# Layer one of two MLP layers: f tiles of two blocks in another order, and three more pairs of them by seven products

## The chip, the cores and the metric

One of the cores of a Trainium2 chip runs the whole program. A core has engines that each work through their own list of instructions in order: TensorE (PE in the profile; PEld is its weight load), VectorE (DVE), ScalarE (ACT), GpSimd (POOL) and SyncE (SP, which here issues DMAs). They wait for each other by semaphores. The metric is the device time of one execution in microseconds, less is better.

## The reference, cut to what matters

Three stages follow each other, in float32:

```
x = attention(q, k, v, lam)                # 2 batches x 768 tokens x 512
u = x + real(fft(fft(x, axis=tokens), axis=features))
un = layernorm(u)
u = u + relu(un @ w1) @ w2                 # layer one, w1 512x2048, w2 2048x512
xn = layernorm(u) * g
out = u + relu(xn @ w1b) @ w2b             # layer two, same sizes
```

The attention is a retention with a decaying state over 12 chunks of 64 tokens (the kernel goes by chunks of 128). The change touches layer one alone.

## The kernel before, in words

Numbers are kept as pairs of float16 (a high part and the rest), so a product of two matrices is three passes of matmuls. The tokens are cut in four blocks of 384: block 0 and 1 are batch 0, block 2 and 3 batch 1 (the two halves of a batch come out of one transform by symmetry). The Fourier step is done by matmuls with tables: for batch 1, `ps_pq1_0` to `ps_pq1_2` hold its results for the token tiles 0 to 2; L594 and L596 are its last matmuls for a tile, L631 adds them to `u`.

A layer goes over its blocks in turn, and in a block over 16 f tiles of 128 hidden features. One unit of the program is one f tile of one block: the up-projection of tile f (`w1`), the relu, and the down-projection (`w2`) of the tile that was begun LAG = 3 units earlier, which adds to three accumulators `ps_y` of 128x512 in PSUM for the whole block. The last tile of a block closes the accumulators (`stop`, in `down_mm`) and adds them to `u` (`drain`, L1021).

The up-projection has two forms:

- The slow form, `mlp_up` (L745 to L756): 12 matmuls of 384 columns for one f tile (L755), so 24 for two tiles. Then ACT takes the relu to float16 (L769) and DVE the rest (L770), once for each tile.
- Seven products, `mlp_up_fast` and `pair_prod` (L842 to L909, all matmuls on L864): two f tiles are taken together as a 2x2 block product, 7 products of 6 matmuls of 192 columns. It needs sums of weights (`sw`, `w1_sums`, L788 to L800) and of the block's input (`th`, `un_sums`, L806 to L839: two `tr` by L811, four DVE operations on `ts`, the casts L828 on ACT and the rests L829 on POOL, all of it twice, for kk = 0 and 1). It also needs work between the products, in PSUM: ACT copies the first product (L880), DVE forms `u2` (L881) and `u3` (L888) and adds (L889, L894, L895); then two relu on ACT (L900) and two rests on DVE (L901). Two of these bind the order. After `u3` has been read out of the left bank's second half (L888), that half is overwritten by the next product:

```
prod(left[:, HB:TB], 3, 3)
prod(left[:, :HB], "12", "21")
dve.tensor_tensor(u3, left[:, HB:TB], m1, op=ALU.add)                  # L888
dve.tensor_tensor(right[:, HB:TB], right[:, :HB], u3, op=ALU.add)      # L889
def rest():                                                            # after the unit's down-projection
    prod(left[:, HB:TB], "22", 4)
```

In layer one, `fast_from` says from which f tile on a block goes by seven products: none of blocks 0 and 1, block 2 from f = 4 (F02), block 3 from 0. All of layer two goes by them.

The input of a block comes from the layer norm: DVE takes statistics (L689, L692, L695), POOL a power (L697), DVE the shift (L708), ACT normalises (L709) and casts (L717), POOL forms the rest (L718), and SP issues the DMA transposes of both parts into `unT` (L720).

`put(n, task)` places such side work at unit n of the program. What each engine does in which order is settled when the program is built: the tile framework's timeline scheduler goes by the order in which the code was written as priority and by its own estimate of durations. At run time each engine keeps that order.

Of the kernel before, what the change touches and what calls it, by code (L numbers as in the profile page):

```python
# [19 lines left out]
P = 128  # L20
# [4 lines left out]
NF = DF // P  # L25
# [23 lines left out]
e0 M12 N12 M20 M21 N20 r0 e1 e0 f0 M22 N21 r1 f0 N22 r2  # L49
"""  # L50
ONPOOL = "Y2"
EARLY0, GATEN, B1, SPC, DS, DC, DFO, DD, D1S, D2S, AO, YA, NR, NE, LN1, L1, L2, F01, F02, TL, R1, R2, SE, PR1, LAG, UB, FB, NW, MQ, SPL = 11, 8, 6, 2.0, 2.0, 5, 1.0, 0.5, 0.5, 1.0, "aba", "aa", 2, 0, 3, 2.5, 2.5, 16, 4, 3, 1.5, 2, "dddd_dppp", 0, 3, 3, 13, 11, 1, 3

SUMS = {(1, 0): 16, (1, 1): 18, (2, 0): 20, (2, 1): 25, (3, 0): 35, (3, 1): 38, (0, 0): 41, (0, 1): 43}

# [71 lines left out]
def tile_retention_fourier_mlp(ctx: ExitStack, tc: tile.TileContext, a: dict, out: bass.AP):  # L127
    nc = tc.nc
    pe, act, dve, pool, sp = nc.tensor, nc.scalar, nc.vector, nc.gpsimd, nc.sync
# [673 lines left out]
    def un_sums(m, blk, kk):  # L803
        run(un_sum_steps(m, blk, kk))

    def un_sum_steps(m, blk, kk):  # L806
        x = unT[m, blk]
        r = []
        for k in (kk, kk + 2):
            t = f32t(f"tr{m}_{blk}_{k}")[:, :TB]  # L810
            dve.tensor_tensor(t, x[:, 0, k], x[:, 1, k], op=ALU.add)  # L811
            yield t
            r += [t[:, :HB], t[:, HB:]]
        b11, b12, b21, b22 = r
        both = [f32t(f"ts{y}_{m}_{blk}_{kk}")[:, :TB] for y in (12, 34)]
        (t1, t2), (t3, t4) = ((z[:, :HB], z[:, HB:]) for z in both)
        tw[m, blk, kk] = []

        def pair(y):
            z = both[y]  # L820
            if (m, blk) == (1, 0):
                t = csp.tile([P, 2, NS], F16, tag=f"cs{2 * kk + y}", name=f"th{y}_{m}_{blk}_{kk}")[:, :, :TB]
            elif (m, blk) == (1, 2):
                t = tops[1 + y].rearrange("p n two -> p (n two)") if kk else wtp.tile([P, 512], F32, tag="wt", name=f"th{y}_{m}_{blk}_{kk}").bitcast(F16)
                t = t.rearrange("p (y n) -> p y n", y=2)[:, :, :TB]
            else:
                t = hl(f"th{y}_{m}_{blk}_{kk}")[:, :, :TB]
            act.copy(t[:, 0], z)  # L828
            pool.tensor_tensor(t[:, 1], z, t[:, 0], op=ALU.subtract)  # L829
            tw[m, blk, kk].append(t)  # L830

        dve.tensor_tensor(t1, b12, b11, op=ALU.subtract)
        yield t1
        dve.tensor_tensor(t2, b22, t1, op=ALU.subtract)
        pair(0)
        yield t2
        dve.tensor_tensor(t3, b22, b12, op=ALU.subtract)
        yield t3
# [72 lines left out]
    def down_mm(m, blk, f, part, first=0):  # L911
        j, c, ps = part
        h, w = hts[m, blk, f], w2t[m, f]
        for n, (x, y) in enumerate(PASS):
            pe.matmul(ps, h[:, x, j * P:(j + 1) * P], w[:, y, c], start=f == first and n == 0, stop=f == NF - 1 and n == 2,  # L915
                      skip_group_check=True)

    vsum, hsum, acc = {}, {}, {}
# [28 lines left out]
    def seven_mm(m, blk, f):  # L947
        p = f // 2
        h, w = [hts[m, blk, 2 * p + i] for i in range(2)], [w2t[m, 2 * p + i] for i in range(2)]
        one, two = slice(0, P), slice(TB - P, TB)  # L950
        (t1, t2), (t3, t4) = ([z[:, :, c] for c in (LEFT, RIGHT)] for z in vsum[p])
        (_, _, c1), (_, _, c2) = dn[blk][:2]
        ca, cb = acc["a"], acc["b"]
        if f % 2 == 0:
            todo = [(ca, LEFT, h[0][:, :, one], w[0][:, :, LEFT], 1), (c1, LEFT, h[1][:, :, one], w[1][:, :, LEFT], 1),
                    (c2, LEFT, h[1][:, :, two], t4, 1)]
        else:
            (s1, s2), (s3, s4) = ([z[:, :, x * P:x * P + P] for x in range(2)] for z in hsum.pop((blk, p)))
            todo = [(ca, RIGHT, s1, t1, 0), (cb, LEFT, s2, t2, 1), (cb, RIGHT, s3, t3, 0), (c1, RIGHT, s4, w[1][:, :, RIGHT], 0)]
        for ps, c, lhs, rhs, start in todo:  # L960
            for n, (x, y) in enumerate(PASS):
                pe.matmul(ps[:, c], lhs[:, x], rhs[:, y], start=start == 1 and n == 0 and p == 0, stop=n == 2,  # L962
                          skip_group_check=True)
        down_mm(m, blk, f, dn[blk][2])
# [42 lines left out]
    def mlp_down(m, blk, f):  # L1007
        if f == 0:
            dn[blk] = [(j, WHOLE, bank("dn", f"ps_y{m}_{blk}_{j}")) for j in range(3)]
        for part in dn[blk]:  # L1010
            down_mm(m, blk, f, part)
        if f == NF - 1:
            for i in range(3):
                drain(m, blk, i)

    def drain(m, blk, i):
        b, mir = divmod(blk, 2)
        j, _, ps = dn[blk][i]
        u = U[b][mir * 3 + j]
        if m == 0:  # L1020
            dve.scalar_tensor_tensor(u, ps, YS, u, op0=ALU.mult, op1=ALU.add)  # L1021
            return
        o = f32t(f"o{blk}_{j}")
        dve.scalar_tensor_tensor(o, ps, YS, u, op0=ALU.mult, op1=ALU.add)
        if not mir:
            sp.dma_start(out[b, j * P:(j + 1) * P, :], o)
            return
        od = dram.tile([P, DM], F32, name=f"od{blk}_{j}")
        sp.dma_start(od, o)
        n0 = 1 if j == 0 else 0  # L1030
# [292 lines left out]
    with tc.manual_schedule(engines={mybir.EngineType.PE, mybir.EngineType.DVE, mybir.EngineType.Pool, mybir.EngineType.Activation}):  # L1323
        for z in ORDER.split():
# [3 lines left out]
            if z[0] == "W":  # L1328
                ps = bank("up", f"warm{len(warm)}")
# [18 lines left out]
    def put(n, task):  # L1348
        bg.setdefault(max(int(n), 0), []).append((n, len(bg), task))
# [27 lines left out]
    n = t + DC + DFO  # L1377
# [11 lines left out]
    order = [[0, 1, 2, 3], [0, 1, 3, 2]]  # L1389
# [14 lines left out]
    first = {}  # L1404
# [18 lines left out]

    def step(n):
        m = n // (NB * NF)
        return m, order[m][n // NF % NB], n % NF

    fast_from = {(0, 2): F02, (0, 3): 0}
    fast_from.update({(1, blk): 0 for blk in range(NB)})
    for (m, blk), f in fast_from.items():  # L1430
        if (m, blk) in ((1, 3), (1, 2)):
            continue
        for kk in range(2):
            if m == 0 and blk < 3:
                put(16 * blk + f / 2 + kk - 3, lambda blk=blk, kk=kk: un_sums(0, blk, kk))
            else:
                at = m * NB * NF + order[m].index(blk) * NF
                put(at - TL + 2 * kk if (m, blk) != (1, 0) else at - 7 + 2 * kk, lambda m=m, blk=blk, kk=kk: un_sums(m, blk, kk))
# [3 lines left out]
    def unit(n):  # L1442
        rest = None
        if n < total:
            m, blk, f = step(n)
            if n >= SPL:
                rest = (mlp_up if f < fast_from.get((m, blk), NF) else mlp_up_fast)(m, blk, f)
        for _, _, task in sorted(bg.pop(n, ()), key=lambda z: z[0]):
            after("dve", lambda: after("act", task)) if n < GATEN else task()
        if n >= LAG:  # L1450
            mlp_down(*step(n - LAG))
        if rest:
            rest()
# [31 lines left out]
```

## Time and profile before

| | |
|---|---|
| three runs | 583.88, 584.0, 584.85 us (median 584.0) |
| profiled execution | 584.66 us |
| its span on the core | 582.8 us |
| mean granted clock of TensorE | 0.997 |
| busy: PE, DVE, ACT, POOL | 97%, 70%, 51%, 59% |

The span is from the first to the last instruction in the trace; what lies around it is 584.66 - 582.8 = 1.86 us. Layer one's block 1 takes its last f tiles at about 190 to 227 us of the span; block 2 begins at 222.55 us, its first pair by seven products ends at about 247 us.

### The profile page before, as it was taken

What the parts mean: (1) busy time and instruction counts of PE and PEld (TensorE: products, weight loads), DVE (VectorE), ACT (ScalarE), POOL (GpSimd) and SP (SyncE); (2) the same over time, 40 slices, a digit from 0 to 9 for tenths busy, and PEclk for the clock granted to TensorE, in tenths of its full rate; (3) what the DMA queues carried; (4) which work ended last, traced back from release to release, by engine and by line L of the source; (5) the groups of instructions that cost most, each with busy time, mean ns of one, the idle gap of its engine ahead of it and who ended that gap; (6) DMA issues with size and microseconds to landing.
All of it is one profiled execution on the core that took longest, in us unless ns stands there. A gap on an engine that the chain in (4) does not pass through costs nothing.

```text
span 582.8 us, 12205 instructions
## 1 busy us (share of the span) xinstructions
PE 564.2 (97%) x4718; PEld 384.5 (66%) x4718; DVE 405.3 (70%) x921; ACT 299.1 (51%) x608; POOL 344.4 (59%) x368
## 2 busy tenths in 40 slices
PE   7879999999999999999999899999999999999997
PEld 4745654666554555677677667666777788878884
DVE  6898798867876449678677766656756665756544
ACT  3657779743232333465597888954242453223320
POOL 8925699995553565365366877754196676223511
PEclk9998999999999999999999999999999999999999
DMA  8999079960000011243365454400120025002001
GB/s 283 374 400 340 2 250 251 339 200 29 1 0 1 10 38 26 75 128 109 83 181 172 133 179 128 140 19 2 56 55 1 19 90 56 1 2 78 34 1 55
DMA packets 47017, 63.26 MB, mean 109 GB/s; under 512 B 26224, under 2 KB 29166, under 8 KB 46958
## 3 DMA queue, kind: packets, MB, share of 16 engines
q1 hardware_dynamic: 46142, 62.27, 34.4%
q8 instruction: 37, 0.61, 0.5%
q10 hardware_dynamic: 816, 0.21, 0.2%
q14 instruction: 22, 0.18, 0.1%
HBM read 52.23 MB, written 6.29 MB: 100 GB/s over the span
## 4 chain that ended last, share of the span: by engine, by line
PE 62%; DVE 13%; POOL 12%; ACT 6%; issue 6%; DMA 1%; SPq 0%; DVEq 0%; POOLq 0%; ACTq 0%
PE ps_y L915 25%; PE ps L864 21%; PE ps_h L755 5%; POOL w L332 4%; POOL m L382 3%; PE ps_y L962 2%; DVE wr L788 1%; PE ps_d L554 1%; POOL kd L344 1%; PE ps_b L962 1%; PE ps_a L962 1%; PE ps_h L745 1%; DVE tr L811 1%; POOL sw L800 1%; DMA qt<-in_qt 1%
## 5 line engine op out<-in xcount | busy, mean ns | idle before, releaser
L915 PE MATMUL ps_y<-w,h 128*128 128x512 f16 (+1 forms) x1026 | 248.1, 377 | 1.8 <-ACT h L900 1.2
L915 PEld LDWEIGHTS <-h 128*128 128x128 f16 x1032 | 98.2, 98 | 88.8 <-ACT h L900 2.5
L864 PEld LDWEIGHTS <-sw 128*128 128x128 f16 x1104 | 94.6, 98 | 20.5 <-issue 2.6
L864 PE MATMUL ps<-th,sw 128*128 128x192 f16 x756 | 86.0, 246 | 1.6 <-DVE wf L307 0.7
L332 POOL TENSOR_TENSOR w<-wf,w 128x512 f16<-128x512 f32 x58 | 66.9, 1160 | 26.7 <-ACT w L330 26.5
L864 PEld LDWEIGHTS <-w 128*128 128x128 f16 x828 | 71.0, 98 | 11.1 <-issue 0.2
L755 PE MATMUL ps_h<-unT,w 128*128 128x384 f16 x396 | 72.3, 326 | 0.7 <-ACT w L330 0.7
L864 PE MATMUL ps<-unT,w 128*128 128x192 f16 x552 | 61.9, 246 | 0.0
L755 PEld LDWEIGHTS <-w 128*128 128x128 f16 x396 | 37.7, 98 | 29.3 <-ACT w L330 1.5
L800 POOL TENSOR_TENSOR sw<-ws,sw 128x512 f16<-128x512 f32 x32 | 37.0, 1174 | 21.2 <-ACT sw L799 21.2
L330 ACT CAST w<-wf 128x512 f16<-128x512 f32 x58 | 35.4, 612 | 12.9 <-DVE wf L317 9.9
L1150 ACT ACTIVATE h<-ps 128x384 f16<-128x384 f32 x44 | 21.7, 496 | 34.6 <-DVE ps L1157 30.0
L307 DVE SCALAR_TENSOR_TENSOR wf<-ws,ps_w 128x512 int32<-128x512 int32 x34 | 23.2, 684 | 17.3 <-ACT ps_w L305 6.9
L697 POOL TENSOR_TENSOR rs<-rs,neghalf 128x1 f32<-128x1 f32 x24 | 14.3, 600 | 35.2 <-DVE rs L695 32.4
L829 POOL TENSOR_TENSOR th<-ts,th 128x384 f16<-128x384 f32 x22 | 20.5, 952 | 24.0 <-ACT th L828 24.0
L901 DVE SCALAR_TENSOR_TENSOR h<-ps,h 128x384 f16<-128x384 f32 x48 | 25.6, 553 | 12.7 <-ACT h L900 12.2
L1179 POOL TENSOR_TENSOR hh<-s,hh 128x256 f16<-128x256 f32 x22 | 14.4, 676 | 32.9 <-ACT hh L1178 30.9
L382 POOL TENSOR_TENSOR m<-m,m 128x512 f16<-128x512 f32 x24 | 30.8, 1300 | 4.5 <-ACT m L380 4.5
L718 POOL TENSOR_TENSOR uns<-un,uns 128x512 f16<-128x512 f32 x21 | 25.2, 1199 | 12.9 <-ACT uns L717 12.9
L900 ACT ACTIVATE h<-ps 128x384 f16<-128x384 f32 x48 | 22.4, 487 | 19.6 <-DVE ps L894 16.0
L770 DVE SCALAR_TENSOR_TENSOR h<-ps_h,h 128x384 f16<-128x384 f32 x36 | 19.7, 548 | 18.2 <-ACT h L769 18.2
L864 PE MATMUL ps<-unT,sw 128*128 128x192 f16 x276 | 30.3, 246 | 0.0
(222 smaller groups left out, 1039.0 us busy)
## 6 DMA issues: line engine op xcount, KB each, us to landing
ws<-in_w SPq DMA_DIRECT2D x25, 511.8 KB, 5.0
ws<-in_w2b SPq DMA_DIRECT2D x16, 511.8 KB, 3.8
ws<-in_w1b SPq DMA_DIRECT2D x16, 511.8 KB, 4.1
kt<-in_kt SPq DMA_DIRECT2D x12, 256.0 KB, 6.6
qt<-in_qt SPq DMA_DIRECT2D x12, 256.0 KB, 5.6
v<-in_v SPq DMA_DIRECT2D x12, 256.0 KB, 5.3
k<-in_k SPq DMA_DIRECT2D x12, 256.0 KB, 4.8
pre<-in_w SPq DMA_DIRECT2D x4, 511.8 KB, 7.5
```

The costliest lines, as they stand in the source:

```text
L307: dve.scalar_tensor_tensor(ti, raw[:, :, 0], 13, part.bitcast(I32), op0=ALU.logical_shift_right, op1=ALU.bitwise_or)
L330: act.copy(hi, t)
L332: gate["lo"] = pool.tensor_tensor(lo, t, hi, op=ALU.subtract)
L382: pool.tensor_tensor(t[:, 1], m32, t[:, 0], op=ALU.subtract)
L718: pool.tensor_tensor(s_[:, 1], un, s_[:, 0], op=ALU.subtract)
L755: pe.matmul(ps, w[:, i, k, fo:fo + P], x[:, j, k, :], start=n == 0, stop=n == 11)
L800: pool.tensor_tensor(lo, z, hi, op=ALU.subtract)
L864: pe.matmul(ps, lhs, rhs, start=start and n == 0, stop=n == 5, skip_group_check=True)
L900: gate["relu"] = act.activation(hi, z, AF.Relu)
L901: dve.scalar_tensor_tensor(lo, z, 0.0, hi, op0=ALU.max, op1=ALU.subtract)
L915: pe.matmul(ps, h[:, x, j * P:(j + 1) * P], w[:, y, c], start=f == first and n == 0, stop=f == NF - 1 and n == 2, skip_group_check=True)
L962: pe.matmul(ps[:, c], lhs[:, x], rhs[:, y], start=start == 1 and n == 0 and p == 0, stop=n == 2, skip_group_check=True)
```

## The change

Three things.

- A function `turn(m, blk)` gives the order of the f tiles. In layer one, block 1 takes 0 to 3, 8 to 15, 4 to 7, and block 2 takes 0, 1, 4 to 15, 2, 3. `last_f` names the tile that comes last, for the stop of the accumulators and the drain.
- `fast_from` counts positions, not tiles. Block 1 goes by seven products from position 12 on (the pairs f 4/5 and 6/7), block 2 from position 2 on (F02 is 2), so that f 2/3, its last pair, is by seven products too. That is three pairs more.
- The sums of block 1's input are new (units 25 and 26 of the program; its `th` tiles lie in `wt` buffers and in `tops`), and those of block 2 stand at units 30 and 31 instead of 31 and 32.

```diff
-            elif (m, blk) == (1, 2):
+            elif (m, blk) in ((0, 1), (1, 2)):
                 t = tops[1 + y]... if kk else wtp.tile([P, 512], F32, tag="wt", ...).bitcast(F16)
...
-            pe.matmul(ps, h[...], w[:, y, c], start=f == first and n == 0, stop=f == NF - 1 and n == 2,
+            pe.matmul(ps, h[...], w[:, y, c], start=f == first and n == 0, stop=f == last_f(m, blk) and n == 2,
...
-        if f == NF - 1:
+        if f == last_f(m, blk):
             for i in range(3):
                 drain(m, blk, i)
...
-        return m, order[m][n // NF % NB], n % NF
-
-    fast_from = {(0, 2): F02, (0, 3): 0}
+        blk = order[m][n // NF % NB]
+        return m, blk, turn(m, blk)[n % NF]
+
+    def turn(m, blk):
+        if (m, blk) == (0, 1):
+            return [*range(4), *range(8, NF), *range(4, 8)]
+        return [0, 1, *range(4, NF), 2, 3] if (m, blk) == (0, 2) else range(NF)
+
+    def last_f(m, blk):
+        return turn(m, blk)[-1]
+
+    fast_from = {(0, 1): 12, (0, 2): F02, (0, 3): 0}
...
-                put(16 * blk + f / 2 + kk - 3, lambda blk=blk, kk=kk: un_sums(0, blk, kk))
+                put(16 * blk + f + kk - (4 if f == 2 else 3), lambda blk=blk, kk=kk: un_sums(0, blk, kk))
...
-                rest = (mlp_up if f < fast_from.get((m, blk), NF) else mlp_up_fast)(m, blk, f)
+                rest = (mlp_up_fast if n % NF >= fast_from.get((m, blk), NF) else mlp_up)(m, blk, f)
```

F02 goes from 4 to 2 in the table of numbers. TensorE has 4503 matmuls in its list instead of 4449 (3 times 42 less 24). The DMAs are the same ones.

The order of TensorE's list where block 1 ends, before, from the last transform matmul of batch 1 (L594) to block 2's first up-projection. In the names the first digit behind `ps_h`, `ps_10`, `ps_20`, `h` is the layer, then block, then tile or pair; `unT0_2` is the input of block 2.

```order
L594 MATMUL ps_pq1_2_2875<-cdsd_1943,cst1_1_2686 128x128
...
L755 MATMUL ps_h0_1_14_2976<-unT0_1_1212,w1_0_3_1403 128x384 [waits DVE_49]
...
L915 MATMUL ps_y0_1_0_2390<-w2_0_11_1620,h0_1_5_2778 128x512
...
L755 MATMUL ps_h0_1_15_3001<-unT0_1_1212,w1_0_3_1403 128x384 [waits DVE_49]
...
L915 MATMUL ps_y0_1_0_2390<-w2_0_12_1706,h0_1_6_2925 128x512
...
L755 MATMUL ps_h0_2_0_3041<-unT0_2_2784,w1_0_0_690 128x384 [waits DMAHW3_49]
```

Between the first and the last of these rows stand 24 matmuls of 384 columns and 36 of 512. The same place in the changed list:

```order
L594 MATMUL ps_pq1_2_2905<-cdsd_1943,cst1_1_2686 128x128
...
L864 MATMUL ps_10_1_4_2943<-th1_0_1_0_2726,sw0_1_0_1_2108 128x192 [waits DVE_49]
...
L915 MATMUL ps_y0_1_2_2392<-w2_0_15_1959,h0_1_7_2794 128x512
...
L864 MATMUL ps_10_1_4_2943<-th1_0_1_0_2726,w1_0_1_1057 128x192 [waits DVE_49]
...
L864 MATMUL ps_10_1_6_3033<-th1_0_1_0_2726,sw0_1_0_1_2108 128x192 [waits DVE_49]
...
L915 MATMUL ps_y0_1_0_2390<-w2_0_4_1168,h0_1_2_3027 128x512
...
L755 MATMUL ps_h0_2_0_3139<-unT0_2_2814,w1_0_0_690 128x384 [waits PE_49]
...
L864 MATMUL ps_10_1_6_3033<-th1_0_1_0_2726,w1_0_1_1057 128x192 [waits DVE_49]
```

Behind L594 stand 12 matmuls of 192 columns and 2 of 512, then the product that overwrites the left half bank of pair f 4/5 (`ps_10_1_4` from `th1` and `w1`; it waits for L888). Up to block 2's first matmul there are 36 of 192 and 9 of 512. The rest of pair 6/7 stands behind that block's first f tile.

The order of DVE's list at the same place, before: the end of the layer norm of block 2's last token tile (and of two tiles of block 3), then the second half of the relu of f 15, statistics, and the input sums of block 2.

```order
L695 TENSOR_SCALAR rs0_3_1_3243<-mv0_3_1_3241 128x1
L708 SCALAR_TENSOR_TENSOR rs0_2_2_2900<-mv0_2_2_2898,rs0_2_2_2900 128x1
L708 SCALAR_TENSOR_TENSOR rs0_3_0_3126<-mv0_3_0_3124,rs0_3_0_3126 128x1
L708 SCALAR_TENSOR_TENSOR rs0_3_1_3243<-mv0_3_1_3241,rs0_3_1_3243 128x1
L770 SCALAR_TENSOR_TENSOR h0_1_7_2989<-ps_h0_1_15_3001,h0_1_7_2989 128x384
L689 BN_STATS bst0_3_2_3421<-u1_120 128x6
...
L811 TENSOR_TENSOR tr0_2_0_3016<-unT0_2_2784 128x384
L811 TENSOR_TENSOR tr0_2_2_3018<-unT0_2_2784 128x384
```

The changed list there:

```order
L708 SCALAR_TENSOR_TENSOR rs0_3_1_3351<-mv0_3_1_3349,rs0_3_1_3351 128x1
L888 TENSOR_TENSOR t0_1_5_3001<-ps_10_1_4_2943,s0_1_4_2942 128x192
L889 TENSOR_TENSOR ps_20_1_4_2944<-ps_20_1_4_2944,t0_1_5_3001 128x192
L894 TENSOR_TENSOR ps_10_1_4_2943<-ps_10_1_4_2943,s0_1_4_2942 128x192
L881 TENSOR_TENSOR s0_1_6_3032<-ps_10_1_6_3033,s0_1_6_3032 128x192
...
L689 BN_STATS bst0_3_2_3529<-u1_120 128x6
...
L811 TENSOR_TENSOR tr0_2_0_3055<-unT0_2_2814 128x384
```

The operations of pair f 4/5 that work in PSUM (L888 to L895) and L881 of pair 6/7 stand behind the whole layer-norm chain. Further on in the same list, those of pair 6/7 stand among the input sums of block 2:

```order
L839 TENSOR_TENSOR ts34_0_2_0_3060<-tr0_2_2_3057,ts12_0_2_0_3059 128x192
L692 BN_AGGR mv1_0_2_4068<-bst1_0_2_4066 128x2
L888 TENSOR_TENSOR t0_1_7_3092<-ps_10_1_6_3033,s0_1_6_3032 128x192
L811 TENSOR_TENSOR tr0_2_1_3095<-unT0_2_2814 128x384
L811 TENSOR_TENSOR tr0_2_3_3097<-unT0_2_2814 128x384
L889 TENSOR_TENSOR ps_20_1_6_3034<-ps_20_1_6_3034,t0_1_7_3092 128x192
L832 TENSOR_TENSOR ts12_0_2_1_3099<-tr0_2_1_3095 128x192
...
L894 TENSOR_TENSOR ps_10_1_6_3033<-ps_10_1_6_3033,s0_1_6_3032 128x192
```

In the list before, the kk = 1 sums (the two L811 and what follows) stood in the same place behind L692, with one L770 among them and nothing of a pair by seven products until the first of block 2.

## Rows read from the trace of the kernel before

**Rows 1.** The page: busy time by engine; the chain that ended last.

```profile
PE 564.2 (97%) x4718; PEld 384.5 (66%) x4718; DVE 405.3 (70%) x921; ACT 299.1 (51%) x608; POOL 344.4 (59%) x368
...
PE 62%; DVE 13%; POOL 12%; ACT 6%; issue 6%; DMA 1%; SPq 0%; DVEq 0%; POOLq 0%; ACTq 0%
```

**Rows 2.** Busy time by stretch: length, PE, PEld, DVE, ACT, POOL; PEclk, DMA share, GB/s.

```profile
54.60:58.00 3.40, 3.17 (x20) 2.70 (x21) 2.50 (x8) 2.41 (x5) 0.56 (x1) 0.51 0.84 292
178.00:192.00 14.00, 14.00 (x79) 6.53 (x78) 7.39 (x15) 4.96 (x12) 3.70 (x3) 1.00 0.00 0
205.00:222.00 17.00, 17.00 (x99) 8.93 (x98) 8.49 (x25) 5.14 (x13) 8.91 (x12) 1.00 0.14 33
222.00:245.00 23.00, 23.00 (x157) 14.23 (x156) 18.05 (x46) 10.15 (x19) 12.24 (x12) 1.00 0.18 52
```

**Rows 3.** Timeline of TensorE: start, length, line, operation, tiles, count.

```profile
202.09 2.11 PE L755 MATMUL ps_h<-unT,w 128*128 128x384 f16 x12
204.04 1.67 PE L915 MATMUL ps_y<-w,h 128*128 128x512 f16 x7
...
300.87 0.66 PE L864 MATMUL ps<-unT,w 128*128 128x192 f16 x6
...
301.86 0.81 PE L915 MATMUL ps_y<-w,h 128*128 128x512 f16 x3
```

**Rows 4.** Timeline of TensorE where block 2 begins.

```profile
210.88 2.11 PE L755 MATMUL ps_h<-unT,w 128*128 128x384 f16 x12
...
216.72 5.99 PE L915 MATMUL ps_y<-w,h 128*128 128x512 f16 x27
222.55 0.65 PE L755 MATMUL ps_h<-unT,w 128*128 128x384 f16 x3
```

**Rows 5.** Timeline of DVE, layer norm of block 2's last token tile.

```profile
211.08 0.76 DVE L631 SCALAR_TENSOR_TENSOR u<-ps_pq,u 128x256 f32<-128x256 f32 x2 [1.52 <-PE ps_pq L594]
211.87 1.88 DVE L689 BATCH_NORM_STATS2 bst<-u 128x6 f32<-128x512 f32 x3
...
213.81 0.52 DVE L770 SCALAR_TENSOR_TENSOR h<-ps_h,h 128x384 f16<-128x384 f32 x1
214.25 0.17 DVE L692 BATCH_NORM_AGGREGATE mv<-bst 128x2 f32<-128x6 f32 x1
...
216.16 0.16 DVE L708 SCALAR_TENSOR_TENSOR rs<-mv,rs 128x1 f32<-128x1 f32 x1 [0.36 <-POOL rs L697]
```

**Rows 6.** Timeline of DVE, two short operations of a pair by seven products.

```profile
242.03 0.36 DVE L888 TENSOR_TENSOR t<-ps,s 128x192 f32<-128x192 f32 x1 [3.25 <-PE ps L864]
242.43 0.37 DVE L889 TENSOR_TENSOR ps<-ps,t 128x192 f32<-128x192 f32 x1
```

**Rows 7.** Timelines of ACT and POOL, and the tile `uns`: the transposes' input.

```profile
216.17 0.62 ACT L717 CAST uns<-un 128x512 f16<-128x512 f32 x1
216.86 1.16 POOL L718 TENSOR_TENSOR uns<-un,uns 128x512 f16<-128x512 f32 x1 [0.74 <-ACT uns L717]
DMA to landing us min/median/max: 2.3/2.3/2.3
```

**Rows 8.** Timeline of DVE, statistics and the input sums of block 2.

```profile
219.41 1.88 DVE L689 BATCH_NORM_STATS2 bst<-u 128x6 f32<-128x512 f32 x3 [1.32 <-POOL u L670]
221.21 1.01 DVE L811 TENSOR_TENSOR tr<-unT 128x384 f32<-128x384 f16 x2
...
222.36 0.33 DVE L832 TENSOR_TENSOR ts<-tr 128x192 f32<-128x192 f32 x1
...
224.23 1.71 DVE L811 TENSOR_TENSOR tr<-unT 128x384 f32<-128x384 f16 x2
225.86 1.07 DVE L832 TENSOR_TENSOR ts<-tr 128x192 f32<-128x192 f32 x1
```

**Rows 9.** Timelines of ACT and POOL, casts and rests of the sums.

```profile
223.64 1.12 ACT L828 CAST th<-ts 128x384 f16<-128x384 f32 x2 [6.13 <-DVE ts L834]
224.23 2.48 POOL L829 TENSOR_TENSOR th<-ts,th 128x384 f16<-128x384 f32 x2 [0.79 <-ACT th L828]
```

More of the change, by code (lines that the diff above doesn't have):

```diff
@@ L51 @@
 ONPOOL = "Y2"
-EARLY0, GATEN, B1, SPC, DS, DC, DFO, DD, D1S, D2S, AO, YA, NR, NE, LN1, L1, L2, F01, F02, TL, R1, R2, SE, PR1, LAG, UB, FB, NW, MQ, SPL = 11, 8, 6, 2.0, 2.0, 5, 1.0, 0.5, 0.5, 1.0, "aba", "aa", 2, 0, 3, 2.5, 2.5, 16, 4, 3, 1.5, 2, "dddd_dppp", 0, 3, 3, 13, 11, 1, 3
+EARLY0, GATEN, B1, SPC, DS, DC, DFO, DD, D1S, D2S, AO, YA, NR, NE, LN1, L1, L2, F01, F02, TL, R1, R2, SE, PR1, LAG, UB, FB, NW, MQ, SPL = 11, 8, 6, 2.0, 2.0, 5, 1.0, 0.5, 0.5, 1.0, "aba", "aa", 2, 0, 3, 2.5, 2.5, 16, 2, 3, 1.5, 2, "dddd_dppp", 0, 3, 3, 13, 11, 1, 3
 SUMS = {(1, 0): 16, (1, 1): 18, (2, 0): 20, (2, 1): 25, (3, 0): 35, (3, 1): 38, (0, 0): 41, (0, 1): 43}
@@ L914, in down_mm @@
         for n, (x, y) in enumerate(PASS):
-            pe.matmul(ps, h[:, x, j * P:(j + 1) * P], w[:, y, c], start=f == first and n == 0, stop=f == NF - 1 and n == 2,
+            pe.matmul(ps, h[:, x, j * P:(j + 1) * P], w[:, y, c], start=f == first and n == 0, stop=f == last_f(m, blk) and n == 2,
                       skip_group_check=True)
```

## The prediction

> **What bounds the kernel now.** First the busy times and the chain: TensorE (PE) works 564.2 of 582.8 us, no other engine over 70%, and the chain that ended last is 62% PE [rows 1]. Then the stretches around the change: from 205 to 222 us and from 222 to 245 us PE is busy all the time, at a granted clock of 1.00 [rows 2]. So here a matmul less is worth its duration, and a wait that PE gets is lost in full, since nothing behind it has idle time worth naming to take it up. Last the timelines, for prices and for what the other engines do while PE is covered.
>
> Prices on PE, from start to start: 12 matmuls of 384 columns take 204.04 - 202.09 = 1.95 us, 0.1625 each; 12 of 192 take 301.86 - 300.87 = 0.99, 0.0825 each [rows 3]; 27 of 512 take 222.55 - 216.72 = 5.83, 0.216 each [rows 4].
>
> **The saving.** A pair was 24 x 0.1625 = 3.90 us and becomes 42 x 0.0825 = 3.465. Three pairs: 3 x 0.435 = 1.3 us less PE work.
>
> **Work that is added elsewhere.** Each pair brings DVE five operations of about 0.36 (L888 and its like, [rows 6]), 1.8 us, and ACT one copy; L900 and L901 stand for L769 and L770. Block 1's sums add two pairs of L811 (1.01 a pair, [rows 8]) and eight operations of 0.33, 4.7 us of DVE, two pairs of casts on ACT (1.12) and two of rests on POOL (2.48, [rows 9]). They run where DVE has 7.39 of 14 us busy, ACT 4.96 and POOL 3.70, from 178 to 192 us [rows 2]: room enough, so I cost them at nothing. If they push the transform's operands back, which stand behind them on DVE, PE would wait at about 188 us; at worst 1 us, within the range.
>
> **First place: the end of block 1.** The pair that was covered by other work is now itself what PE has left. Count from the first matmul behind the last L594, 210.88 in the trace of before [rows 4]. In the changed list PE has 12 matmuls of 192 and 2 of 512 before the product that overwrites the half bank read by L888: 12 x 0.0825 + 2 x 0.216 = 1.42 us. L888 stands on DVE behind the layer norm of block 2's last token tile. That chain cannot begin before the same L594 (its L631 starts at 211.08, released by it), and it ended with the third L708 at 216.16 + 0.16 = 216.32 [rows 5], 5.44 us after our zero; one L770 within it is gone, 214.25 - 213.81 = 0.44, which leaves 5.00. With L888 of 0.36 [rows 6], 5.36, and a few hundredths for the signal: 5.4. PE stalls 5.4 - 1.42 = 4.0 us. In the chain DVE itself waits for POOL (0.36 before the last L708), so that no faster DVE would mend it. Behind it PE has 12 matmuls (1.0 us) until it needs L881 of pair 6/7, which comes after L889 and L894 and a copy on ACT behind L709 and L717: about 0.1 more. First place: 4.1 us, 3.5 to 4.5 by how much of the chain the removed L770 truly shortens.
>
> In the trace of before the same chain was as long, but PE had 24 x 0.1625 + 36 x 0.216 = 11.7 us of independent work beside it [rows 4].
>
> **Second place: block 2's sums against pair 6/7.** DVE's statistics at 219.41 waited for POOL (L670), which hangs on the same layer norm, and lasted with block 2's first sums until 224.23 [rows 8]; in the changed kernel 0.44 earlier, 218.97 to 223.79 on the clock of before. Then come L888 of pair 6/7, the two L811 of kk = 1, and only then L889. The row prices this pair of L811 at 1.71 and the L832 behind it at 1.07 where POOL ran L829 beside them, 1.01 and 0.33 where it did not [rows 8, 9]. POOL's L829 of kk = 0 move with the rest, so I take the long values: L811 from 224.1, L889 done at about 226.0, L832 and L834 at 227.3, the cast L828 (0.56) at 227.9, POOL's rest (1.24) at 229.1, and two matmuls later, 229.3, PE gets to the down-projection of pair 6/7. PE's own work from 210.88 to there is 60 x 0.0825 + 20 x 0.216 + 12 x 0.1625 = 11.2 us, which without any wait ends at 222.1. The difference, 7.2 us, is what both places cost together: 4.1 at the first, 3.1 at the second (behind L889 1.2, the cast 1.3, POOL's rest 0.6). With the short values the end is at 227.9 and the sum 5.8. Both places hang on one layer norm, so a longer first stall shortens the second; their sum is the safer number.
>
> The pair of L811 beside POOL's L829 took 0.70 us longer than alone [rows 8, 9]. The Trainium skill (SBUF — State Buffer, "SBUF: two separate sides") says that VectorE with two inputs in SBUF and GpSimd take a shared port as an exclusive lock for a whole instruction; by that, each L811 could wait out a whole L829, 2.48 us for both in place of 0.70, and the sum would be 1.8 us higher. The trace shows much less, and it decides.
>
> **Third place: block 2's pair f 2/3.** It replaces slow matmuls of the same block by 0.435 us less work, amid other pairs with three units of down-projection as cover; no term but the saving. Block 2's first pair now comes two tiles sooner, beside DVE's busiest stretch (18.05 of 23 us, [rows 2]); a few tenths either way.
>
> **Sum.** -1.3 + 7.2 = +5.9. The profiled execution took 584.66 us (span 582.8 and 1.86 around it), so 590.6 by its own time; it was 0.66 above the median 584.0, so 589.9 on the scale of the medians.
>
> **Rivals.**
>
> 1. Only the first place binds, as DVE gets block 2's sums done sooner than I think. Then -1.3 + 4.1 gives 586.8. Its floor is the transposes: the high part's cast ended at 216.79 and lands 2.3 later [rows 7], 218.65 with the 0.44 off, while PE's 36 x 0.0825 + 9 x 0.216 = 4.9 us end at 215.8: 2.9 us of wait even without L888, so 585.6. For it: the short L811. Against it: PE then reaches L889, cast and rest only sooner.
> 2. Neither place binds and the saving is all: 582.7, faster. It would take a layer norm that is not behind PE's last transform matmul, or waits of both places below 1.3 us together, where now one chain of 5.0 us meets 1.42 us of cover. For it: each unit before 205 us had such a chain covered. Against: the row's releaser, PE L594, and the list's order. Waits between 0.1 and 2.5 us in all would read as no change.
> 3. The clock. From 54.6 to 58.0 us the granted clock was 0.51, 1.2 GHz instead of 2.4, with PE busy 3.17 of the 3.40 us [rows 2]; half speed there cost at most 3.17 / 2 = 1.6 us. Should a stall of 4 us bring such a stretch, it costs up to 1.6; if it falls between the two places, the second wait swallows it, as its end is set by DVE and POOL; behind the second it is lost: 591.5. The Trainium skill (TensorE: Matmul & The Clock Gate, "HAM oscillation — how this bites in real kernels") says that a TensorE left idle falls back to half clock and pays after each gap; by that the upper number is the one to expect. No stall of this size stands in these rows, so they leave it open.
>
> That the change does not do what it says is excluded by the 54 more matmuls in the list.
>
> **How the numbers follow.** The forecast, both places at 5.8 to 7.2 us (588.5 to 589.9, with a few tenths of either sign): 0.57. Rival 1 (585.6 to 588): 0.18. Rival 3 (590.5 to 591.8): 0.12. Rival 2: 0.07 faster, and 0.06 for waits that just eat up the saving. About 0.2%, 1.2 us, is what a measurement of this kernel can tell from no change. Slower: 0.57 + 0.18 + 0.12 = 0.87. The range takes in rival 1's floor and rival 3's end, 585.6 to 591.8; what is left out is rival 2 and half of no change.
>
> **What the profile after would show.** A gap on PE of about 4 us before a product of `th` and `w` on L864, near 212 to 216 us, released by DVE L888 or its neighbour; about 3 us of gaps in the next 15 us released by DVE L889, ACT L828 or POOL L829; PE's busy sum lower by about 1.3 us; a granted clock of 1.00 through both, or a dip if rival 3 holds. I am wrong if the gaps there come to less than 2.5 us, if they end on a DMA (rival 1's floor), or if PE waits more elsewhere, above all at the transform near 188 us.

## The result, and the profile after

The changed kernel takes 592.93 us (median of 5, 592.63 to 594.22), the kernel before 584.85 (median of 5, 583.88 to 585.5): a ratio of 1.0146, interval 1.0132 to 1.0159. It is slower, as forecast, but by 8.1 us where 5.9 were forecast, and outside the range (591.8). The spans of the two profiled executions, 591.1 and 582.8 us, differ by 8.3.

The page of the changed kernel: span, busy time by engine, and the chain that ended last.

```profile
span 591.1 us, 12356 instructions
PE 565.8 (96%) x4772; PEld 389.2 (66%) x4772; DVE 417.1 (71%) x948; ACT 301.3 (51%) x615; POOL 348.5 (59%) x372
...
PE 56%; DVE 15%; POOL 14%; issue 7%; ACT 6%; DMA 2%; SPq 0%; POOLq 0%; DVEq 0%; ACTq 0%
```

PE's busy time did not fall by the 1.3 us saved; against [rows 1] it grew, which the granted clock explains in part (below). Busy time by stretch, columns as in [rows 2]:

```profile
178.00:192.00 14.00, 13.29 (x71) 6.06 (x69) 13.46 (x27) 6.09 (x13) 8.42 (x7) 1.00 0.00 0
212.00:218.00 6.00, 2.27 (x26) 1.66 (x24) 3.82 (x16) 1.30 (x2) 2.98 (x6) 1.00 0.00 0
218.00:224.00 6.00, 5.77 (x34) 3.77 (x34) 4.39 (x10) 1.66 (x6) 2.52 (x3) 0.72 0.81 48
228.00:233.00 5.00, 3.15 (x30) 2.34 (x28) 4.54 (x12) 2.12 (x5) 2.77 (x3) 1.00 0.00 0
```

Three stretches that were full in [rows 2] have holes now, and from 218 to 224 us the granted clock is 0.72 on the mean. PE's timeline from the first matmul behind the last L594 on (it answers to [rows 4]):

```profile
212.67 0.25 PE L864 MATMUL ps<-th,sw 128*128 128x192 f16 x1
...
213.66 0.59 PE L915 MATMUL ps_y<-w,h 128*128 128x512 f16 x2
217.99 0.24 PE L864 MATMUL ps<-th,w 128*128 128x192 f16 x1 [3.73 <-DVE t L888]
...
219.35 0.32 PE L864 MATMUL ps<-th,sw 128*128 128x192 f16 x1 [0.15 <-DVE s L881]
...
229.74 0.66 PE L864 MATMUL ps<-unT,sw 128*128 128x192 f16 x6 [1.06 <-DVE ps L889]
231.01 0.82 PE L864 MATMUL ps<-th,sw 128*128 128x192 f16 x8 [0.61 <-ACT th L828]
232.00 0.33 PE L864 MATMUL ps<-th,sw 128*128 128x192 f16 x2 [0.17 <-POOL th L829]
232.16 0.59 PE L915 MATMUL ps_y<-w,h 128*128 128x512 f16 x2
```

Both places are there, with the releasers that the prediction named: L888 and L881, then L889, the cast L828 and POOL's L829. From 212.67 to 232.16 are 19.49 us for 11.2 us of work, so 8.3 are lost. From start to start, the gaps are 217.99 - 213.66 - 2 x 0.216 = 3.9, then 0.4, 1.2, 0.8 and 0.3, together 6.6; the other 1.7 are matmuls at half clock (0.72 over 6 us is 3.4 us at 1.2 GHz). These are PE's losses where they lie in its list. What they hang on is read from DVE.

DVE in the same stretch (it answers to [rows 5, 8]):

```profile
217.50 0.16 DVE L708 SCALAR_TENSOR_TENSOR rs<-mv,rs 128x1 f32<-128x1 f32 x1 [0.36 <-POOL rs L697]
217.58 0.35 DVE L888 TENSOR_TENSOR t<-ps,s 128x192 f32<-128x192 f32 x1
...
220.76 1.88 DVE L689 BATCH_NORM_STATS2 bst<-u 128x6 f32<-128x512 f32 x3
223.85 1.03 DVE L811 TENSOR_TENSOR tr<-unT 128x384 f32<-128x384 f16 x2 [1.21 <-DMA unT<-uns]
...
227.12 2.29 DVE L811 TENSOR_TENSOR tr<-unT 128x384 f32<-128x384 f16 x2
229.33 0.35 DVE L889 TENSOR_TENSOR ps<-ps,t 128x192 f32<-128x192 f32 x1
229.60 0.34 DVE L832 TENSOR_TENSOR ts<-tr 128x192 f32<-128x192 f32 x1
```

L888 runs right behind the third L708. From here on times are counted from PE's first matmul behind the last L594 (212.67 in this trace, 210.88 in that of before). The statistics (L689) begin after 220.76 - 212.67 = 8.09 us, where the forecast had 218.97 - 210.88 = 8.09 too: up to there the half clock has held up nothing on DVE. Then the kk = 0 pair of L811 waits 1.21 us for block 2's transposes, which landed 4.4 us after their issue and not 2.3 as in [rows 7]. It begins after 11.18 us, where the forecast had 221.21 - 0.44 - 210.88 = 9.89, and every wait of the second place hangs on what follows it. The kk = 1 pair of L811, beside POOL's L829, takes 2.29 us, not 1.71; the L832 behind it takes 0.34 us, not 1.07. And a third place, at the transform, which I had costed at nothing:

```profile
186.59 1.31 DVE L837 TENSOR_TENSOR ts<-tr,tr 128x192 f32<-128x192 f32 x1
187.82 0.41 DVE L796 TENSOR_TENSOR ws<-wr,ws 128x256 f32<-128x256 f32 x1
188.15 0.35 DVE L834 TENSOR_TENSOR ts<-tr,ts 128x192 f32<-128x192 f32 x1
188.42 1.01 DVE L571 SCALAR_TENSOR_TENSOR cst<-ps_d,cst 128x384 f16<-128x384 f32 x2
```

```profile
187.50 0.81 PE L755 MATMUL ps_h<-unT,w 128*128 128x384 f16 x4
189.02 1.14 PE L554 MATMUL ps_d<-cs,fhl 128*128 128x385 f16 x6 [0.71 <-DVE cst L571]
```

PE waits there until L571, behind block 1's sums on DVE, has read out a bank: 189.02 - 187.50 - 4 x 0.1625 = 0.87 us. The account: -1.3 saved, +6.6 of gaps, +1.7 of half clock, +0.87 at the transform, and 0.2 more at block 2's first pair: 8.1 where the spans differ by 8.3. A third of a microsecond was already there at 162 us, ahead of everything the change touches, so the sum is open by one or two tenths.

### The profile page after: what moved, and what is told of

It is laid out like the page before. It is cut to its first block, busy times and chain, and to the rows that moved or that the text cites. A ratio compares the mean times of both kernels' runs of the same rounds, so it can differ in the third digit from the quotient of the medians.

```text
span 591.1 us, 12356 instructions
## 1 busy us (share of the span) xinstructions
PE 565.8 (96%) x4772; PEld 389.2 (66%) x4772; DVE 417.1 (71%) x948; ACT 301.3 (51%) x615; POOL 348.5 (59%) x372
## 4 chain that ended last, share of the span: by engine, by line
PE 56%; DVE 15%; POOL 14%; issue 7%; ACT 6%; DMA 2%; SPq 0%; POOLq 0%; DVEq 0%; ACTq 0%
PE ps_y L915 23%; PE ps L864 23%; POOL w L332 4%; POOL m L382 3%; PE ps_y L962 2%; POOL sw L800 1%; POOL kd L344 1%; PE ps_h L755 1%; DVE tr L811 1%; PE ps_b L962 1%; PE ps_a L962 1%; PE ps_h L745 1%; ACT w L330 1%; DVE ts L832 1%; DMA qt<-in_qt 1%
## 5 line engine op out<-in xcount | busy, mean ns | idle before, releaser
L864 PEld LDWEIGHTS <-sw 128*128 128x128 f16 x1176 | 101.0, 98 | 24.4 <-issue 6.0
L864 PE MATMUL ps<-th,sw 128*128 128x192 f16 x792 | 91.6, 246 | 2.9 <-DVE s L881 1.1
L864 PEld LDWEIGHTS <-w 128*128 128x128 f16 x882 | 76.0, 98 | 15.8 <-issue 4.2
L864 PE MATMUL ps<-unT,w 128*128 128x192 f16 x588 | 66.5, 247 | 0.0
L755 PE MATMUL ps_h<-unT,w 128*128 128x384 f16 x324 | 60.1, 326 | 0.9 <-ACT w L330 0.8
L755 PEld LDWEIGHTS <-w 128*128 128x128 f16 x324 | 30.6, 98 | 25.3 <-ACT w L330 1.7
L1150 ACT ACTIVATE h<-ps 128x384 f16<-128x384 f32 x44 | 21.7, 496 | 34.6 <-DVE ps L1157 30.0
L829 POOL TENSOR_TENSOR th<-ts,th 128x384 f16<-128x384 f32 x24 | 23.2, 988 | 27.1 <-ACT th L828 27.1
L901 DVE SCALAR_TENSOR_TENSOR h<-ps,h 128x384 f16<-128x384 f32 x54 | 28.9, 554 | 11.8 <-ACT h L900 11.3
L864 PE MATMUL ps<-th,w 128*128 128x192 f16 x264 | 31.6, 246 | 3.8 <-DVE t L888 3.7
L900 ACT ACTIVATE h<-ps 128x384 f16<-128x384 f32 x54 | 25.4, 487 | 17.4 <-DVE ps L894 14.1
L864 PE MATMUL ps<-unT,sw 128*128 128x192 f16 x294 | 32.5, 246 | 1.1 <-DVE ps L889 1.1
```

Of the source, the lines that this page charges most:

```text
L755: pe.matmul(ps, w[:, i, k, fo:fo + P], x[:, j, k, :], start=n == 0, stop=n == 11)
L864: pe.matmul(ps, lhs, rhs, start=start and n == 0, stop=n == 5, skip_group_check=True)
L900: gate["relu"] = act.activation(hi, z, AF.Relu)
L901: dve.scalar_tensor_tensor(lo, z, 0.0, hi, op0=ALU.max, op1=ALU.subtract)
```

## The experiments

Every kernel below is an edit of the changed kernel; times are medians on the device, ratios are against the kernel before, run on the same chip.

**Only block 2's pair.**

```diff
-        if (m, blk) == (0, 1):
-            return [*range(4), *range(8, NF), *range(4, 8)]
...
-    fast_from = {(0, 1): 12, (0, 2): F02, (0, 3): 0}
+    fast_from = {(0, 2): F02, (0, 3): 0}
```

> Block 1 as before the change (16 slow f tiles in their old order); only block 2's pair f 2/3 is by seven products, at its end, with block 2's sums one unit earlier. Theory A (all of the loss lies where block 1 ends and where its sums run): the saving of one pair, -0.43 us, with a few tenths of either sign, so 0.0 to -0.8 us against before, and no stall of PE over 1 us between 180 and 235 us. Theory B (the earlier sums of block 2 and its first pair at DVE's busiest stretch cost much): 2 to 3 us slower than before.

587.40 us, 1.0046 (1.0034 to 1.0058). Theory A missed: block 2's single pair costs 2.5 us by itself. No stall stands between 180 and 235 us; it lies at block 2's first pairs. Timelines of DVE, ACT and PE:

```profile
235.46 1.28 DVE L788 TENSOR_TENSOR wr<-w 128x512 f32<-128x512 f16 x2
236.66 0.36 DVE L894 TENSOR_TENSOR ps<-ps,s 128x192 f32<-128x192 f32 x1
...
237.05 0.49 ACT L900 ACTIVATE h<-ps 128x384 f16<-128x384 f32 x1 [4.86 <-DVE ps L894]
...
237.60 0.61 PE L915 MATMUL ps_y<-w,h 128*128 128x512 f16 x2 [0.84 <-ACT h L900]
```

DVE does 1.28 us of weight sums ahead of L894, ACT waits for L894, PE for ACT. It is the mechanism of the first place with other work at the head of the list; whether it is all of the 2.5 us, block2_weights_later asks.

**Only block 1's two pairs.**

```diff
-        return [0, 1, *range(4, NF), 2, 3] if (m, blk) == (0, 2) else range(NF)
+        return range(NF)
```

(with F02 at 4 and block 2's sums where they were)

> Block 2 as before the change; only block 1 has the new order and its two pairs by seven products at its end. Theory A (the loss is block 1's alone): 8.0 to 8.7 us slower than before, with the 3.7 us stall released by DVE's L888 near 218 us, and the 0.9 us gap of the transform near 188 us. Theory B (block 2 has a part): 5 to 6 us slower.

591.89 us, 1.0126 (1.0111 to 1.0141): 6.9 us, between the two theories. The stall for L888 (217.05, idle 3.73) and the gap at 188 us are there. 6.9 and 2.5 make 9.4, more than the 8.1 of both: the parts do not add up. Each of them gives DVE another list, which may be why; no run shows it.

**Block 3's statistics held back.**

```diff
-    ln_tasks(0, 3, 34, 3)
+    ln_tasks(0, 3, 34, 3, lambda task: behind_pair(task))   # DVE: behind block 1's last L901
```

> The changed kernel with one edit: on DVE the layer-norm statistics of block 3's three tokens tiles, which nothing needs yet, are queued behind the last relu of block 1 (issue order only). Theory A (the first stall is DVE's layer-norm chain, of which two thirds belong to block 3): two of three statistics and two of three powers go, 2.1 us shorter up to L888, so the first stall falls from 3.7 to about 1.6 us; the statistics also go from the second place, whose 2.3 us become 1.2 to 1.5; 2.5 to 5 us faster than the changed kernel, 588 to 590.5. Theory B (PE waits for L888 because of something else, such as block 2's own tile or the transposes): within 0.5 us of the changed kernel.

589.57 us, 1.0092 (1.0074 to 1.011), 3.4 us faster than the change. PE's timeline and two stretches of it:

```profile
212.74 0.59 PE L915 MATMUL ps_y<-w,h 128*128 128x512 f16 x2
214.98 0.24 PE L864 MATMUL ps<-th,w 128*128 128x192 f16 x1 [1.65 <-DVE t L888]
...
217.16 0.32 PE L864 MATMUL ps<-th,sw 128*128 128x192 f16 x1 [1.02 <-DVE s L881]
```

```profile
217.00:223.00 6.00, 5.84 (x23) 3.21 (x23) 3.74 (x11) 1.24 (x4) 1.83 (x4) 0.50 0.23 45
```

The first stall fell from 3.9 to 1.8 us, as theory A said, and the second place is gone; a new wait of 1.2 us for L881 came up, and PE then ran at half clock for all of 6 us. The clock differs between executions: the six had mean granted clocks of 1.000, 0.997, 0.994, 0.994, 0.991 and 0.991 and took 588.86, 588.84, 589.27, 589.87, 591.65 and 591.99 us. The profiled one is that of 589.87 us; why the last two took 2 us more, no trace shows.

**The pairs in the middle of block 1.**

```diff
-            return [*range(4), *range(8, NF), *range(4, 8)]
+            return [*range(4), *range(8, 12), *range(4, 8), *range(12, NF)]
```

(seven products at positions 8 to 11, sums at units 21 and 22)

> The changed kernel with block 1's order 0 to 3, 8 to 11, 4 to 7, 12 to 15: the two pairs f 4/5 and 6/7 by seven products stand at positions 8 to 11, and four slow tiles stand behind them again, at the layer norm of block 2; the sums of block 1 come at units 21 and 22, before the transform's folds. Theory A (the loss is the missing cover behind the last transform matmul, and the sums before the transform's operands): the stall of L888 near 218 us and the two of the second place are gone, 583 to 586 us, so 6 to 9 us faster than the changed kernel. Theory B (block 1's seven products cost DVE and ACT time wherever they stand): 589 us or more.

593.18 us, 1.0156 (1.0134 to 1.0177): as slow as the change. There is no stall behind the last L594; PE waits at other places, 1.6 us at block 1's own pairs from 197 to 200 us and more at block 2's:

```profile
253.00 1.24 PE L915 MATMUL ps_y<-w,h 128*128 128x512 f16 x3 [2.12 <-ACT h L900]
```

Cover behind the layer norm alone does not rescue the change. Theory B's number came, though by several places of one kind and not by one price.

**The stall filled with matmuls.** Results that nobody reads, into 128 unused columns of a bank:

```diff
+                with tc.issue_after(gate["down"].ins):          # behind f 15's last L915
+                    for _ in range(64):
+                        pe.matmul(left[:, TB:512], lhs, rhs, start=True, stop=True, skip_group_check=True)
```

> The changed kernel with 64 matmuls of 128 columns, whose results nobody reads, put on PE where it stalls for L888 (into the unused columns of pair 6/7's bank; block 1's f 15 goes through its down-projection a little sooner to make this possible). They last about 3.6 us, no longer than the stall, so PE stays busy through it. Theory A (the half clock after the stall is lost on top of the stalls): the granted clock stays at 1.00 from 218 to 224 us and the time falls by 1.5 to 2 us, to about 591. Theory B (the end of the second place is set by DVE and the transposes, so the second wait swallows the slow clock): the clock stays at 1.00, the waits between 224 and 232 us grow by 1.5 to 2 us, and the time is within 0.5 us of the changed kernel.

591.28 us, 1.0113 (1.0099 to 1.0128), 1.65 us faster than the change. Its stretches:

```profile
212.00:218.00 6.00, 5.91 (x93) 5.57 (x91) 3.95 (x16) 1.43 (x3) 2.91 (x5) 1.00 0.01 3
218.00:224.00 6.00, 5.78 (x44) 3.81 (x43) 5.55 (x17) 1.53 (x5) 2.52 (x3) 1.00 0.20 45
```

The clock stays at 1.00, so the half clock comes of the stall, and more matmuls made the kernel faster. The time falls by what theory A said, but this does not show that the half clock is a loss on top of the stalls, for a second thing differs: the transposes landed 2.3 us after their issue, not 4.4. PE's first matmul behind the last L594, and DVE:

```profile
212.54 0.25 PE L864 MATMUL ps<-th,sw 128*128 128x192 f16 x1
```

```profile
220.63 1.88 DVE L689 BATCH_NORM_STATS2 bst<-u 128x6 f32<-128x512 f32 x3
222.43 1.01 DVE L811 TENSOR_TENSOR tr<-unT 128x384 f32<-128x384 f16 x2
```

L689 begins 220.63 - 212.54 = 8.09 us behind that matmul, as in the changed kernel with its half clock. L811 begins after 9.89 us, as forecast, and not after 11.18. So 1.3 of the 1.6 us between the two spans (591.1 and 589.5) are DVE's wait for the DMA. The order of PE's list also differs a little, as block 1's f 15 goes down sooner.

**PE's code shifted.**

```diff
-                for _ in range(int(z[1:])):
-                    pe.matmul(ps[:, :2 * P], ident.bitcast(F16)[:, :P], ident.bitcast(F16), start=True, stop=True)
+                for _ in range(4 * int(z[1:])):
+                    pe.matmul(ps[:, :P // 2], ident.bitcast(F16)[:, :P], ident.bitcast(F16)[:, :P // 2], start=True, stop=True)
```

> The changed kernel with PE's warm-up matmuls near 35 us (18 of 256 columns in all) cut into 72 of 64 columns: the same columns, 54 matmuls and their weight loads more in PE's list. This moves by 108 instructions the places at which PE's code is fetched; in the changed kernel two such fetches fell in the same microsecond as the last transposes of block 2's input, whose low part landed 4.4 us after its issue in place of 2.3. Theory A (the fetches delay the transposes): the landing is 2.3 to 3.0 us again, DVE's wait for it at 223.85 us (1.2 us) goes, and the time falls by 0.5 to 1.3 us. Theory B (the late landing comes from the stall or the place itself): 4 us or more again, and the same time within 0.4 us.

592.93 us, 1.0138 (1.0125 to 1.0151): the same time as the change. The landing of block 2's last transposes, in the changed kernel and in this one, and this one's PE and DVE:

```profile
DMA to landing us min/median/max: 4.4/4.4/4.4
```

```profile
DMA to landing us min/median/max: 2.8/2.8/2.8
```

```profile
212.17 0.25 PE L864 MATMUL ps<-th,sw 128*128 128x192 f16 x1
```

```profile
218.62 0.37 DVE L894 TENSOR_TENSOR ps<-ps,s 128x192 f32<-128x192 f32 x1 [0.79 <-PE ps L864]
...
219.58 0.37 DVE L895 TENSOR_TENSOR ps<-ps,s 128x192 f32<-128x192 f32 x1 [0.34 <-PE ps L864]
...
222.76 1.01 DVE L811 TENSOR_TENSOR tr<-unT 128x384 f32<-128x384 f16 x2
```

So the landing moved as theory A said, and the time did not, by the medians. But the execution with the trace took 591.79 us, 1.1 less than that of the changed kernel; the other three took 592.92 to 592.98, and when their transposes landed is not known. In the trace L811 waits for no DMA and begins after 10.59 us: 0.6 sooner than in the changed kernel, 0.7 later than in filled_stall. The 0.7 I put down to the half clock, which here came sooner: the granted clock was 0.51 from 218 to 221 us, and L894 and L895 of pair 4/5, ahead of block 2's sums on DVE, waited 0.79 and 0.34 us for PE's slow products. The rest of the 1.1, half a microsecond, lies ahead of 212.17. So the late landing held DVE up by 1.3 us in one execution and the half clock by 0.7 in another. In the changed kernel, which had both, the half clock had held up nothing when the wait for the DMA began. Whether PE's code fetches cause the late landing is not settled by one such shift.

**Block 1's sums later.**

```diff
-                put(16 * blk + f + kk - (4 if f == 2 else 3), ...)
+                put(((26, 27)[kk] if blk == 1 else 16 * blk + f + kk - (4 if f == 2 else 3)), ...)
```

> The changed kernel with one number changed: block 1's input sums are put at units 26 and 27 in place of 25 and 26, by which the kk = 1 half goes on DVE behind the transform's operands (L571), and the kk = 0 half stands one operation nearer to them. Theory A (the gap of 0.87 us at 188 us is these sums ahead of L571): the gap goes or falls below 0.3 us, and with it 0.6 to 0.9 us of the time, unless the later half is late for its first product. Theory B (the gap comes from the transform or POOL): it stays, same time within 0.3 us.

589.79 us, 1.0096 (1.008 to 1.0113). The gap at 188 us is gone:

```profile
178.00:192.00 14.00, 14.00 (x76) 6.33 (x74) 10.79 (x24) 5.16 (x11) 5.49 (x5) 1.00 0.00 0
```

But 3.1 us is far more than the 0.9 expected. The execution with the trace was the slowest of six, 591.89 us, 1.0 less than the changed kernel's; no trace shows a fast one. In it the stall for L888 is 3.4 us in place of 3.9 plus 0.4, as PE's list now has three more matmuls of 512 and six of 192 behind the last L594; what is left of the 3.1 I cannot put to one place.

**Block 2's weight sums later** (with block 1 as before the change).

```diff
-SUMS = {(1, 0): 16, (1, 1): 18, (2, 0): 20, (2, 1): 25, (3, 0): 35, (3, 1): 38, ...}
+SUMS = {(1, 0): 16, (1, 1): 18, (2, 0): 20, (2, 1): 25, (3, 0): 38, (3, 1): 40, ...}
```

> Block 1 as before the change, block 2 with its pair f 2/3 by seven products (as in only_block2), and one edit: the weight sums of group 3 (L788 and what follows) at units 38 and 40 in place of 35 and 38. In DVE's list L894 and L895 of block 2's first pair then stand ahead of them. Theory A (the 2.5 us that block 2's pair cost are DVE's long operations ahead of L894): the waits near 237 and 247 us fall from 3.5 us to about 1.5, and the time is 585 or less, perhaps below the kernel before (583.6 to 585.2). Theory B (block 2's first pair comes too early for DVE whatever stands before it): 587 again.

587.82 us, 1.0056 (1.0044 to 1.0068): no better than only_block2. L894 of the first pair now runs at 236.65 us with no weight sums ahead of it, and the waits come back elsewhere, so L788 ahead of L894 is not what the 2.5 us hang on alone:

```profile
237.98 0.66 PE L864 MATMUL ps<-th,sw 128*128 128x192 f16 x6 [0.87 <-DVE s L881]
...
261.98 0.98 PE L915 MATMUL ps_y<-w,h 128*128 128x512 f16 x3 [1.79 <-ACT h L900]
```

**L888 ahead of the layer norm.** hold_stats, and the statistics of block 2's last tile behind L888:

```diff
+    def behind_u3():
+        with tc.issue_after(gate["u3", 0, 1, 5].ins):      # DVE: behind L888 of pair f 4/5
+            ln_a(0, 2, 2)
```

> As hold_stats (block 3's statistics behind block 1's last relu), and the statistics of block 2's last token tile queued on DVE behind L888 of pair f 4/5 (issue order; its task stands at unit 29 for this). L888 then waits only for PE's own 12 matmuls, about 1.4 us after the last L594, and PE's list puts 15 matmuls of 512 columns ahead of pair 6/7's products. Theory A (the order of DVE's list is what makes the stall, and nothing else is as late): no stall over 0.6 us at the first place, no stretch of half clock behind it, 585.5 to 587.5. Theory B (rival 1's floor: block 2's transposes hold PE 2.9 us in any case): a stall of 2 us or more before block 2's first up-projection, and 588 to 590.

591.22 us, 1.0099 (1.0079 to 1.0119). PE's and DVE's timelines:

```profile
213.34 0.24 PE L864 MATMUL ps<-th,w 128*128 128x192 f16 x1
...
223.22 0.33 PE L864 MATMUL ps<-th,sw 128*128 128x192 f16 x2 [0.87 <-ACT th L828]
...
226.09 0.66 PE L864 MATMUL ps<-unT,sw 128*128 128x192 f16 x6 [1.95 <-DVE ps L889]
```

```profile
212.93 0.36 DVE L888 TENSOR_TENSOR t<-ps,s 128x192 f32<-128x192 f32 x1 [0.23 <-PE ps L864]
...
220.93 1.03 DVE L811 TENSOR_TENSOR tr<-unT 128x384 f32<-128x384 f16 x2 [2.70 <-DMA unT<-uns]
...
223.34 2.41 DVE L811 TENSOR_TENSOR tr<-unT 128x384 f32<-128x384 f16 x2
```

Theory A is right that the order of DVE's list makes the first stall: the product that waited 3.9 us now waits 0.2. Theory B's floor by the transposes is not there either, for PE's list was filled with 15 matmuls of 512. But of the time that this won, much is given back at the second place, whose gaps grew from 2.3 to 3.8 us: DVE waits for the transposes at 220.93, and block 2's sums then stand ahead of L889. Half clock follows there (0.52 from 227 to 230.5 us).

**Both.** pair_first with the sums at 26 and 27.

> As pair_first, with block 1's sums at units 26 and 27 (as in sums_later). If the causes add up (the sums ahead of the transform's operands 0.87 us, the layer norm ahead of L888 and its half clock the rest): 0.6 to 1.2 us faster than pair_first, 584.5 to 586.7, and the change costs at most 2 us against the kernel before. If sums_later won its 3 us by something else, such as fewer stretches of half clock: within 0.4 us of pair_first, or faster than it by over 2 us.

590.33 us, 1.0088 (1.0067 to 1.011): 0.9 us below pair_first, about the gap at 188 us, as if the causes add up there. The two intervals overlap, so the times alone do not show it.

**The rests on DVE.** pair_first, with

```diff
-            pool.tensor_tensor(t[:, 1], z, t[:, 0], op=ALU.subtract)
+            (dve if (m, blk, kk) == (0, 2, 0) else pool).tensor_tensor(t[:, 1], z, t[:, 0], op=ALU.subtract)
```

> As pair_first, with the two rests (L829) of block 2's kk = 0 sums on DVE in place of POOL, so that POOL has nothing beside the kk = 1 pair of L811, which took 2.41 us in pair_first beside those rests and 1.0 us where POOL was idle. Theory A (VectorE and GpSimd wait for each other whole instructions: each L811 ran only when an L829 had ended): that pair of L811 takes 1.0 to 1.2 us again, DVE has two rests of about half a us more, and pair 6/7's L889 comes up to 1 us sooner; 589.7 to 591.2, 0 to 1.5 us faster than pair_first. Theory B (the pair is slow there for another reason): 2 us or more again, and 591 or more.

589.62 us, 1.0094 (1.008 to 1.0108). The median is 1.6 us below that of pair_first, but by the ratios, each to the kernel before on its own chip, the two differ by 0.0005, 0.3 us, well within their intervals. DVE there:

```profile
223.69 1.02 DVE L811 TENSOR_TENSOR tr<-unT 128x384 f32<-128x384 f16 x2
224.62 0.55 DVE L829 TENSOR_TENSOR th<-ts,th 128x384 f16<-128x384 f32 x1
225.09 0.35 DVE L889 TENSOR_TENSOR ps<-ps,t 128x192 f32<-128x192 f32 x1
```

With POOL idle the pair of L811 is back at 1.02 us, as theory A said. DVE got two operations more and still came to L889 0.3 us sooner, 13.6 us behind PE's first matmul (211.48) where pair_first took 13.9. No version tried is faster than the kernel before.

## Why the prediction was right and wrong

- **The saving** of 1.3 us was not measured apart; in the account it fits to a few tenths.
- **First place**: right. L888 stands behind the layer norm: 3.9 us where 4.0 were forecast, and 0.4 behind it where it was 0.1. hold_stats and pair_first show the cause: shorten or move the chain, and the stall goes with it.
- **Second place**: right in its releasers and their order; here a step failed. I let DVE begin block 2's sums right behind its statistics and put block 2's transposes at nothing. Only rival 1 has them, at 2.3 us and for the high part alone. By [rows 7] the low part is ready at 216.86 + 1.16, so at 217.58 with the 0.44 off, and lands at 219.88, in time for L811 at 220.77. With the 4.4 us of the trace it lands at 221.98, 1.21 us late: just the wait that the trace shows. PE came to the down-projection of pair 6/7 19.5 us behind its first matmul, where the forecast had 229.3 - 210.88 = 18.4: 1.3 for the transposes, less 0.2 by the other prices. So both places cost 8.3 us, forecast 7.2. Why the transposes landed late stays open.
- **Rival 3, the clock**: the half clock came behind the first stall, and I gave it 0.12. The Trainium skill's rule (TensorE: Matmul & The Clock Gate, "HAM oscillation — how this bites in real kernels") is that a TensorE left idle comes back at half clock. The trace agrees behind the first stall, with 0.72 from 218 to 224 us, and not behind the gaps of the second place, with 1.00 from 228 to 233. The 1.6 us more that I set against it is not where the miss comes from. I wrote that the second wait swallows a half clock between the two places, and in the changed kernel's trace it does: PE lost 1.7 us, the gaps behind it were 2.3 where 3.1 were forecast, and their end hung on the transposes. My reason was too strong, though. L894, L895 and L901 of pair 4/5 wait for PE's products and stand ahead of block 2's sums, and in shifted_code, where the half clock came sooner, this held DVE up by 0.7 us.
- **Block 1's sums at no cost**: the other step that failed, 0.87 us. I took a mean, 7.39 of 14 us busy, for room; after, DVE is busy 13.46 of 14. The sums stand right ahead of L571, and several took two to four times their price beside POOL (L837 1.31 us). sums_later moves them and the gap goes. I had allowed 1 us in the range and none in the sum.
- **The pair of L811**: the sum of two prices was right, my reading of the row was not. In [rows 8, 9] the pair beside POOL's L829 took 0.70 us longer than alone and the L832 behind it 0.74 longer; I held only the first against the skill's rule. In the changed kernel the pair took 2.29 us and L832 0.34, together 0.15 less than the 1.71 and 1.07 of the forecast. The Trainium skill (SBUF — State Buffer, "SBUF: two separate sides") has VectorE with two SBUF inputs and GpSimd take a port as an exclusive lock. The trace agrees that they wait for each other (1.3 to 1.4 us longer beside L829 than the 1.02 with POOL idle), but the 1.8 us that I worked out from the rule did not come on top.
- **Block 2's pair f 2/3**: I costed it by the saving alone with a few tenths of either sign. In the changed kernel that holds (0.2 us), but only_block2 shows that it was luck: alone it costs 2.5 us at block 2's pairs.

So the direction and the main chain were right. The forecast of 5.9 us missed by 2.2: block 2's transposes with the prices behind them (1.1), the sums ahead of the transform (0.9) and block 2's first pair (0.2). This account is of one execution, which was also the median one. The transform's part is shown by an experiment, that of the transposes by traces alone.

## What to carry to other kernels

A form with fewer matmuls that needs other engines between its products is only worth its saving where those engines' lists let the in-between operations through at once; look at what stands ahead of each in its engine's order, not at the engine's busy share. Give every input of a chain its own time of arrival, the DMA's too, and the room that is left there: here it was 0.9 us. A half clock behind a stall of TensorE is swallowed by a later wait only so far as the later wait's end hangs on nothing that TensorE feeds. A stall removed at one place of a chain is time won only if the next wait hangs on another chain.

## What the runs showed of the hardware that was not expected

- After a stall of 1.8 us and another of 1.2 (hold_stats) TensorE ran 6 us at half clock in the execution with the trace, which took 589.87 us; another of the same kernel had a mean clock of 1.000 and took 588.86.
- 64 matmuls that nobody needs, put into a stall of 3.9 us, kept the granted clock at 1.00 behind it, where it had been 0.72.
- DVE's operations on two SBUF inputs and POOL's keep each other waiting: an L811 of 0.5 us took 1.1 to 1.3 beside L829, and L829 1.2 in place of 0.9.
- The landing of the same pair of DMA transposes took 2.3 us in the kernel before, 2.8 in shifted_code, 3.7 in sums_later and 4.4 in the changed kernel. No run shows why.
